# A hand-ordered kernel of gated linear attention and a rational feed-forward: the list of its 800 steps put into another order

## The chip, the core and the metric

The kernel runs on one core of one Trainium2 chip. A core has four engines that compute, each with an instruction queue of its own that is worked off strictly in order: TensorE (PE in the profile; its weight loads are PEld), VectorE (DVE), ScalarE (ACT) and GpSimd (POOL). SyncE (SP) only issues transfers. Transfers (DMA) are issued from SP's and POOL's queues here and are carried by 16 DMA engines. The metric is the device time of one execution in microseconds; lower is better.

## The reference, cut to what matters

```python
f = 1.0 / (1.0 + np.exp(-f_logit))                   # B, H, S, D = 4, 8, 768, 48
for t in range(S):
    state = f[:, :, t, :, None] * state + np.einsum('bhd,bhe->bhde', k[:, :, t], v[:, :, t])
    y[:, :, t] = np.einsum('bhd,bhde->bhe', q[:, :, t], state)
x = y.transpose(0, 2, 1, 3).reshape(B * S, H * D)    # 3072 x 384
h = x @ w_in                                         # 3072 x 2048
P = a[0] + a[1] * h + a[2] * h**2 + a[3] * h**3
Q = 1.0 + abs(b[0]) * abs(h) + abs(b[1]) * h**2
out = (P / (Q + 1e-06)) @ w_out                      # 3072 x 384
```

## The kernel before

The 3072 rows are cut into 12 units of 256 rows (`unit`; unit n is chunk n // 4 of batch n % 4), so units 0 to 3 are the first chunks of the four batches. A unit goes through an attention part and then through a feed-forward part, whose 2048 columns are handled in 16 blocks of 128 columns.

Nothing is scheduled by a framework. The program is the text constant `ORDER`: a list of steps, in the order in which they are issued, and the loop at the end of the kernel calls one small function for each. A step's number is its unit, the next numbers are a range (head pairs 0 to 4 in the attention part, column blocks 0 to 16 in the feed-forward part), `@n` names which of the four PSUM slots (two banks each) it opens, and a last letter picks the engine. Because each engine works in order, the text fixes the order on every engine; a step starts when the step ahead of it on its engine is through and its inputs have come. Beyond the data dependencies a step can carry `^m`, which makes it wait for the instruction that was named with `!m`. The function `behind` adds that wait. `!m` alone costs nothing.

The steps of the attention part, with the engine that does them:

- `ld n f|k|q|v`: loads; v from POOL's queue, the others from SP's. f, k, q and v have three buffers each, so a load waits until unit n - 3 has let go of the buffer. A load in two halves reads two head pairs at a time.
- `ef`, `ls` (ACT): exp of -f and the logarithm of one plus it (lines 294, 299). `cs` (PE, lines 309 to 317): running sums over the rows of a unit by triangular matrices; it also reads the padding columns of the logarithms, and `ind`. `A` (ACT, line 331): exponentials of these sums, for k (`x` = 1) and for q (`x` = 0).
- `xa n x` (line 336): q or k times A, on DVE, or on POOL with the letter p; half a unit is 128x384, a whole one 128x768.
- `T` (PE, line 350): sixteen transposes into PSUM. `Te` (line 360 on ACT with the letter s; without it the last line of the function, a copy on DVE): takes them out to SBUF.
- `sc` (PE) and `mk` (DVE, line 381): scores and their mask. `ic`, `si` (PE) and `st` (DVE, line 464): the new state. `yi`, `yb` (PE, line 394): the output y from the state and from the scores; `vm` (DVE with v, else POOL, line 388) lays out pieces of v for it. `ye` (ACT with s, line 457; else DVE, line 459): y out of PSUM as x.

The steps of the feed-forward part:

- `wi`, `wo`: the two weights, loaded from POOL's queue; `wi a 8 16` is a quarter of the rows of w_in for the upper eight blocks. `ab_` loads a or b from SP's queue; `fa` (DVE, lines 267 to 275) works out nine small coefficients from b, `fr` reads two of them into ScalarE registers, `fb` scales a.
- `h` (PE, line 480): four blocks of x @ w_in, 12 matmuls. `hy` (ACT, line 492): out of PSUM as bf16.
- `sq` (DVE) or `sa` (ACT, line 501): the square. `ab` (DVE, line 505): the absolute value. `zv` (DVE, line 510) or `zd` (a DMA that adds, issued by POOL, line 514): their sum z. `rq` (ACT, line 519): 1 / (z and constants).
- `p1`, `p2` (DVE, lines 529 and 534): two linear terms of the polynomial, `pm` (DVE, line 539) the product with the square, `tv` (DVE, line 547) or `ta` (an adding DMA issued by POOL, line 543) their sum, `gm` (DVE, line 551) the product with 1/z. Each comes in halves (`0 8`, `8 16`, 128x2048) or whole (`0 16`, 128x4096).
- `o` (PE, line 560): four blocks of the product with w_out for 128 rows. `oe` (ACT, line 568): out of PSUM. `so`: the stores, on SP's queue.

`tab` loads one of ScalarE's two function tables. `cu`, `ci`, `cm`, `cz` make constants: `cz 0` and `cz 1` clear the padding columns of the two sets of buffers (lines 250 to 252), `cz 2` makes `ind`, `cz 3` and `cz 4` make two more. `dm` (PE, line 473) is two matmuls of zeros whose product nothing reads.

The last loop, which turns a line of the text into instructions:

```python
made = steps[name](*(int(x.lstrip("@")) if x.lstrip("@").isdigit() else x for x in args))
made = made if isinstance(made, list) else [made]
if hold is not None:
    for i in made:
        behind(i, hold)
if mark is not None:
    marks[mark] = made[-1]
```

Of the kernel before, what the change touches and what calls it, by code (L numbers as in the profile page):

```python
# [29 lines left out]
hy 0 8 12; yi 1 1; xa 2 0 2 4; yb 1 0 2; ab 0 8 16; ic 2 @3; ye 1 s; T 2 @0; p1 0 8 16 !m5; A 3 1; st 2 0  # L30
h 1 12 16 @1; Te 2 s; sq 0 8 16; A 3 0; ld 4 f; si 2 1; sc 2 1 @0; st 2 1; hy 1 12 16; sc 2 0 @2; p2 0 8 16
ld 3 k; ef 5; h 0 4 8 @3; pm 0 8 16; ls 5; ld 6 f; h 0 0 4 @1; tv 0 8 16; hy 0 4 8; xa 3 0 2 4 p ^m1; mk 2 1
h 1 4 8 @3; ld 4 q; ef 4; ld 3 v ^m4; zv 0 8 16 !m7; hy 0 0 4; yb 2 2 4 @0; ls 4; xa 3 0 0 2 p ^m5; h 1 0 4 @1
mk 2 0; hy 1 4 8; ld 7 f; xa 3 1; yb 2 0 2; ef 6; ld 4 k; yi 2 1; sq 0 0 8; T 3 @2; hy 1 0 4; h 1 8 12 @3
# [595 lines left out]
```

## Time and profile before

| what | value |
|---|---|
| three runs | 216.84, 217.03 and 220.1 us; median 217.03 us |
| the profiled execution | 219.54 us in all, 217.8 us of it the span that the profile shows |
| busy time | PE 194.5, DVE 190.6, ACT 187.5, POOL 78.8 us |
| instructions | PE 2901 matmuls, DVE 243, ACT 178, POOL 98 |
| transfers | 43.15 MB at a mean of 198 GB/s |
| granted TensorE clock, mean | 0.99 |

The profiled execution took 2.5 us longer than the median of the runs, and 1.7 us of it lie outside the span. A busy time is the union of an engine's instructions: on DVE and ACT an instruction starts before the one ahead of it is reported as ended, so a difference between two starts is what an instruction costs on a full engine, and it is a little less than its duration. Matmul ends are modelled, so a busy PE need not be at its peak. The idle time in a row stands before the row's instruction, with the instruction or transfer that ended it.

### The profile page before, as it was taken

The numbers are of one execution on the slowest core, as the hardware profiler recorded it, in microseconds if no ns is written. First come the engines' busy times: TensorE is split into PE (matmuls) and PEld (weight loads), VectorE is DVE, ScalarE is ACT, GpSimd is POOL, SyncE is SP. The second block draws the span as 40 slices with busy tenths as digits, with TensorE's granted clock in tenths as the row PEclk, the third lists the DMA queues.
The fourth block names the chain that finished last, engine by engine and source line by source line (L and its number), as shares of the span: only waits on it lengthen the run. The fifth ranks groups of instructions, "written<-read, shape, count | busy, mean of one in ns | idle before, by whom it ended". The sixth has DMA issues, their size and how long they took to land.

```text
span 217.8 us, 6636 instructions
## 1 busy us (share of the span) xinstructions
PE 194.5 (89%) x2901; PEld 138.5 (64%) x2902; DVE 190.6 (88%) x243; ACT 187.5 (86%) x178; POOL 78.8 (36%) x98
## 2 busy tenths in 40 slices
PE   1397699699988899999999999999999999999791
PEld 0355478477756766666678668768677757765440
DVE  4178549999999999999999999999999999979960
ACT  3863639979989999999999999999999999998921
POOL 7050724116394074070260055193553414132000
PEclk9999889999999999999999999999999999999999
DMA  6999997599899979999999999999999999999722
GB/s 171 232 313 168 253 240 189 66 297 182 217 187 178 163 113 200 223 213 191 253 197 164 257 241 243 210 193 204 215 204 199 221 199 215 207 205 199 158 72 72
DMA packets 61820, 43.15 MB, mean 198 GB/s; under 512 B 51424, under 2 KB 56544, under 8 KB 61792
## 3 DMA queue, kind: packets, MB, share of 16 engines
q0 software_dynamic: 20528, 23.86, 66.9%
q1 hardware_dynamic: 41264, 18.88, 33.2%
q8 instruction: 22, 0.36, 0.6%
q14 instruction: 6, 0.05, 0.1%
HBM read 25.17 MB, written 4.72 MB: 137 GB/s over the span
## 4 chain that ended last, share of the span: by engine, by line
PE 54%; DVE 18%; DMA 13%; ACT 8%; issue 4%; POOL 1%; SPq 0%; DVEq 0%; ACTq 0%
PE op L560 19%; PE hp L480 19%; PE y L394 5%; DMA w_in_sb<-in_moe_w_in_dram 4%; DVE g L539 4%; DMA g<-hy 4%; DMA z<-h 4%; PE tp L350 4%; DVE g L551 3%; PE cs L309 3%; DVE scm L381 2%; DVE hy L534 2%; PE sc L373 2%; DMA f<-in_f_logit_dram 2%; ACT A L331 2%
## 5 line engine op out<-in xcount | busy, mean ns | idle before, releaser
L480 PE MATMUL hp<-x,w_in_sb 128*128 128x256 bf16 x576 | 70.9, 276 | 2.4 <-ACT x L457 1.0
L560 PE MATMUL op<-w_out_sb,g 128*128 128x384 bf16 x384 | 69.2, 326 | 1.8 <-DVE g L551 1.8
L480 PEld LDWEIGHTS <-w_in_sb 128*128 128x128 bf16 x576 | 55.7, 99 | 12.8 <-issue 3.1
L492 ACT CAST hy<-hp 128x1024 bf16<-128x1024 f32 x48 | 48.0, 1026 | 6.9 <-PE hp L480 6.9
L560 PEld LDWEIGHTS <-g 128*128 128x128 bf16 x384 | 35.3, 98 | 25.0 <-DVE g L551 3.2
L519 ACT ACTIVATE qi<-z 128x2048 bf16<-128x2048 bf16 (+1 forms) x20 | 45.3, 2267 | 2.1 <-DMA z<-h 1.9
L543 POOL DMA_DIRECT2D g<-hy x15 | 15.3, 1017 | 50.6 <-DVE hy L534 23.1
L381 DVE TENSOR_TENSOR scm<-sc,mask 128x1024 bf16<-128x1024 f32 x24 | 28.9, 1216 | 4.0 <-PE sc L373 3.9
L551 DVE TENSOR_TENSOR g<-g,qi 128x2048 bf16<-128x2048 bf16 (+1 forms) x22 | 28.8, 1315 | 2.1 <-DMA g<-hy 1.6
L539 DVE TENSOR_TENSOR g<-g,h 128x2048 bf16<-128x2048 bf16 (+1 forms) x22 | 30.4, 1394 | 0.0
L514 POOL DMA_DIRECT2D z<-h x20 | 21.6, 1078 | 21.7 <-DVE z L505 11.6
L501 ACT ACTIVATE h<-hy 128x2048 bf16<-128x2048 bf16 x14 | 27.1, 1934 | 0.0
L331 ACT ACTIVATE A<-cs 128x768 f32<-128x768 f32 (+3 forms) x26 | 19.2, 773 | 1.7 <-PE cs L317 1.6
L534 DVE TENSOR_SCALAR hy<-hy,a_sb 128x2048 bf16<-128x2048 bf16 x24 | 19.9, 834 | 0.3
L336 POOL TENSOR_TENSOR qkp<-k,A 128x384 bf16<-128x384 f32 x12 | 12.1, 1012 | 19.8 <-DVE sig L274 8.0
L529 DVE TENSOR_SCALAR g<-hy,a_sb 128x2048 bf16<-128x2048 bf16 (+1 forms) x22 | 18.9, 862 | 0.2 <-PE op L560 0.2
L505 DVE TENSOR_SCALAR z<-hy 128x2048 uint16<-128x2048 uint16 (+1 forms) x23 | 16.1, 707 | 2.6 <-ACT hy L492 2.6
L212 POOL DMA_DIRECT2D v<-in_v_dram x12 | 12.5, 1042 | 15.4 <-DVE qkp L336 7.0
L309 PE MATMUL cs<-lsp,Ui 128*128 128x384 bf16 (+1 forms) x39 | 11.1, 344 | 6.2 <-ACT lsp L299 6.2
L360 ACT COPY T<-tp 128x1024 f32<-128x1024 f32 (+1 forms) x13 | 12.5, 963 | 4.5 <-PE y L394 3.3
L568 ACT ACTIVATE osb<-op 128x768 f32<-128x768 f32 (+1 forms) x13 | 9.9, 762 | 6.1 <-PE op L560 5.6
L394 PE MATMUL y<-scm,v 64*32 64x128 bf16 x384 | 13.2, 218 | 2.0 <-DVE scm L381 2.0
...
## 6 DMA issues: line engine op xcount, KB each, us to landing
...
out_dram<-osb SPq DMA_DIRECT2D x22, 192.0 KB, 4.2
v<-in_v_dram POOLq DMA_DIRECT2D x12, 192.0 KB, 7.3
w_in_sb<-in_moe_w_in_dram POOLq DMA_DIRECT2D x8, 192.0 KB, 9.0
```

Of the source, the lines that this page charges most:

```text
L331: nc.scalar.activation(t, s["cs", a0][:, :, 0:n1], AF.Exp, scale=1.0 if x else -1.0)
L381: return nc.vector.tensor_mul(t, s["sc", g].rearrange("s r a i t -> s (r a) (i t)"), mb)
L394: nc.tensor.matmul(s["y"][32 * a:32 * a + 32, j, kk * C:kk * C + C].rearrange("e (i t) -> e i t", i=2), lhsT, rhs, start=(j, a) not in s[" ...
L480: nc.tensor.matmul(t[:, m - m0, :].rearrange("f (j t) -> f j t", j=UB), w_in_sb[:, kk, m * P:(m + 1) * P], s["x"][:, :, kk, :], start=(kk ...
L492: nc.scalar.copy(fl(big(s, "hy"), m0, m1), fl(s["hp", m0], 0, m1 - m0))
L501: return nc.scalar.activation(fl(big(s, "h2"), m0, m1), fl(big(s, "hy"), m0, m1), AF.Square)
L514: return nc.gpsimd.dma_start(out=fl(big(s, "z"), m0, m1), in_=fl(big(s, "h2"), m0, m1), accum_op=ALU.add)
L519: return nc.scalar.add_instruction(mybir.InstActivation(name=nc.get_next_instruction_name(), func=AF.Reciprocal, ins=[nc.scalar.lower_ap(f ...
L534: return nc.vector.tensor_scalar(fl(big(s, "hy"), m0, m1), fl(big(s, "hy"), m0, m1), a_sb[:, 1:2], a_sb[:, 0:1], op0=ALU.mult, op1=ALU.add)
L539: return nc.vector.tensor_mul(fl(big(s, "g"), m0, m1), fl(big(s, "g"), m0, m1), fl(big(s, "h2"), m0, m1))
L551: return nc.vector.tensor_mul(fl(big(s, "g"), m0, m1), fl(big(s, "g"), m0, m1), fl(big(s, "qi"), m0, m1))
L560: nc.tensor.matmul(s["op", g][:, j, 0:DM], big(s, "g")[:, m, C * j:C * j + C], w_out_sb[:, m, :], start=(s["on", j] == 1), stop=(s["on", j ...
```

## The change

Only the text `ORDER` changes; no function does. It has 795 steps in place of 813, and no computation of the reference is added or dropped. Four kinds of edit are in it:

- The order of nearly all steps is new, on every engine and on SP's and POOL's queues.
- Some steps run on another engine. `Te` goes from 13 on ACT to 9 on ACT and 4 on DVE (`Te 0 2 4`, `Te 1`, `Te 4`, `Te 10`). `vm` on DVE goes from 7 to 4. Squares: DVE 10 to 9, ACT 14 to 15 halves. z sums: DVE 4 to 5, DMA 20 to 19. g sums: DVE 9 to 8, DMA 15 to 16. `xa` on POOL goes from 22 halves to 21.
- Some pairs of half steps become whole ones: `ab` 1 whole before and 5 after, `p1` 2 and 5, `p2` 0 and 4, `pm` 2 and 3, `gm` 2 and 4, `rq` 4 and 7, `xa` on DVE 1 and 4.
- The waits that are written out go from 31 to 34, and the unread products (`dm`) from 4 to 6. The 34 are put so that no product on POOL (`xa ... p`) is meant to run beside a DVE step between SBUF operands.

The diff, cut to the beginning, the end and the lines with the steps named above:

```diff
@@ -17,88 +17,86 @@
 ORDER = """
-cu 1; cz 2; ld 0 f 2 4; cz 0; ld 1 f; cu 0; cz 4; ld 0 f 0 2; dm 3 @0; ld 0 q 0 2; ci; cm; cz 3; ld 0 v; cz 1
-ef 0 2 4; ld 1 k; ld 0 k 0 2; ld 1 v; ab_ b s; ef 0 0 2; ls 0 0 2; ld 0 q 2 4; ls 0 2 4; ef 1; cs 0 2 4 @1
-cs 0 0 2 @2; A 0 1 2 4; ld 0 k 2 4; A 0 0 0 2; ls 1; xa 0 0 0 2; A 0 0 2 4; cs 1 @3; A 0 1 0 2; ld 2 f
-xa 0 1 0 2 !m0; ld 1 q; T 0 0 2 @0; A 1 1; fa; A 1 0; dm 13 @1; xa 1 1 0 2 p ^m0; Te 0 0 2 s; dm 1 @2
-wi 2 8 16; xa 0 0 2 4; ld 3 f; xa 0 1 2 4; wi 0 8 16; vm 1 v; T 0 2 4 @3; wi 3 8 16; xa 1 1 2 4; wi 1 8 16
-ld 2 k; ab_ a s; ef 2; sc 0 0 @1; dm 10 @0; Te 0 2 4 s; mk 0 0; ls 2; sc 0 1 @2; ic 0 @0; xa 1 0 2 4
-xa 1 0 0 2; mk 0 1 !m3; T 1 @3; st 0 0; ld 2 q; yi 0 1 @1; si 0 1; Te 1 s; cs 2 @2; st 0 1; vm 0 v !m1; fr
-ld 2 v ^m1; yb 0 0 2; ef 3; yb 0 2 4; wi 2 0 8; sc 1 1 @0; ld 5 f; ye 0 s; sc 1 0 @3; wi 3 0 8; mk 1 1 !m2
-ls 3; ic 1 @1; wi 0 0 8; A 2 1; wi 1 0 8; mk 1 0 !m4; h 0 8 12 @0; A 2 0; xa 2 1 0 2 p ^m2; st 1 0; si 1 1
-h 0 12 16 @3; xa 2 1 2 4; ld 3 q; fb; st 1 1; cs 3 @2; hy 0 12 16; vm 2 ^m4; xa 2 0 0 2 p ^m3; yb 1 2 4 @1
...
-o 6 0 0 4; rq 8 0 16; sc 11 0 @1; o 6 1 0 4; mk 11 0; o 7 1 8 12; pm 9 8 16; o 7 0 8 12; yb 11 2 4 @2
-pm 8 0 8; yi 11 0; oe 6 0 2 s; yi 11 1; o 7 0 12 16; rq 9 0 8; p1 9 0 8; so 6 0 2; yb 11 0 2; ta 8 0 8
-p2 9 0 8; h 10 4 8 @1; pm 9 0 8; sa 10 8 16; o 7 1 12 16; ab 10 8 16; o 7 0 0 4; ta 9 0 8; p1 10 8 16
-h 10 0 4 @0; ye 11 s; zd 10 8 16; p2 10 8 16; hy 10 4 8; pm 10 8 16; o 7 1 4 8; hy 10 0 4; o 7 0 4 8
-gm 8 8 16; rq 9 8 16; h 11 12 16 @2; tv 10 8 16; h 11 8 12 @1; oe 7 0 2 s; p2 9 8 16; sa 10 0 8
-o 8 1 12 16 @0; so 7 0 2; gm 8 0 8; ta 9 8 16; h 11 0 4 @3; p1 10 0 8; hy 11 8 12; o 8 1 8 12; ab 10 0 8
-hy 11 12 16; gm 9 0 8; o 8 1 4 8; zd 10 0 8; o 8 0 12 16; sa 11 8 16; pm 10 0 8; o 8 0 8 12; o 8 0 4 8
-ab 11 8 16; o 8 0 0 4; hy 11 0 4; p1 11 8 16; zd 11 8 16; o 9 0 4 8 @1; p2 11 8 16; rq 10 8 16; o 8 1 0 4
-gm 9 8 16; h 11 4 8 @2; p2 10 0 8; o 9 1 0 4; oe 8 0 2 s; pm 11 8 16; o 9 0 0 4; hy 11 4 8; so 8 0 2
-o 9 0 12 16; gm 10 8 16; rq 10 0 8; ta 11 8 16; o 9 0 8 12; ab 11 0 8; o 9 1 8 12; tv 10 0 8; o 9 1 4 8
-sa 11 0 8; o 9 1 12 16; p1 11 0 8; o 10 1 8 12 @3; gm 10 0 8; o 10 0 12 16; oe 9 0 2 s; o 10 0 8 12
-rq 11 8 16; zv 11 0 8; so 9 0 2; o 10 1 4 8; o 10 0 4 8; pm 11 0 8; o 10 0 0 4; rq 11 0 8; gm 11 8 16
-o 10 1 0 4; o 10 1 12 16; p2 11 0 8; o 11 0 8 12 @0; oe 10 0 2 s; tv 11 0 8; o 11 1 8 12 @2; so 10 0 2
-o 11 1 12 16; gm 11 0 8; o 11 0 12 16; o 11 0 0 4; o 11 0 4 8; o 11 1 0 4; oe 11 0 1 s; o 11 1 4 8; so 11 0 1
-oe 11 1 2 s; so 11 1 2
+cu 0; cz 3; ld 0 f 0 2; cz 4; dm 3 @0; ld 0 f 2 4; ci; ab_ b s; ld 1 f; cu 1; ld 0 k 2 4; ld 1 v; ld 0 q 2 4
+ld 0 k 0 2; ld 0 v; ef 0 2 4; ef 0 0 2; fa; ls 0 0 2; ld 1 k; cz 0; ef 1; cz 1; cz 2; ls 0 2 4; ls 1
+cs 0 2 4 @1; ld 1 q; cs 1 @2; A 0 0 2 4; fr; cs 0 0 2 @3; A 1 0; ld 2 f; A 0 1 0 2; A 0 1 2 4; A 1 1
+xa 0 1 2 4; ld 4 f; ld 0 q 0 2; xa 0 1 0 2; A 0 0 0 2; vm 1 v; ic 0 @0; xa 0 0 2 4 !m0; vm 0 ^m0; ld 2 k
+T 0 2 4 @1; st 0 0; wi 1 8 16; xa 1 1 2 4; wi 0 8 16; dm 6 @2; xa 1 0; wi 3 8 16; ld 2 q; ef 2; dm 5 @3
+Te 0 2 4; wi 2 8 16; ab_ a s; ls 2; xa 1 1 0 2; dm 13 @2; cm; sc 0 1 @1; xa 0 0 0 2; T 0 0 2 @3; mk 0 1 !m2
+si 0 1; Te 0 0 2 s; ef 4; sc 0 0 @2; ic 1 @1; mk 0 0; cs 2 @3; st 1 0 !m1; T 1 @2; A 2 1; st 0 1; ld 2 v ^m1
+ld 3 f; A 2 0; yi 0 1 @0; yb 0 2 4; Te 1; wi 3 0 8; ls 4; yb 0 0 2; wi 0 0 8; ld 5 f; si 1 1; ye 0 s; xa 2 1
+wi 2 0 8; sc 1 1 @3; sc 1 0 @2; wi 1 0 8; h 0 8 12 @0; mk 1 1; xa 2 0 0 2 p ^m1; fb; h 0 12 16 @3
+xa 2 0 2 4 p ^m2; hy 0 8 12; st 1 1 !m3; mk 1 0; yi 1 1 @1; hy 0 12 16; T 2 @0; yb 1 2 4; sq 0 8 16; Te 2 s
+ld 3 q; ic 2 @2; yb 1 0 2; st 2 0; sc 2 1 @3; ab 0 8 16; si 2 1; ef 3; cs 4 @0; p1 0 8 16; ye 1 s; st 2 1
+ls 3; vm 2 v !m6; mk 2 1; A 4 1; cs 3 @1; ld 4 q; p2 0 8 16; A 4 0; sc 2 0 @2; zv 0 8 16; A 3 0; yb 2 2 4 @3
+ld 3 k; h 0 0 4 @0; A 3 1; mk 2 0; ef 5; h 0 4 8 @1; ld 4 k; xa 3 0 2 4 p ^m2; hy 0 0 4; ld 3 v; ls 5
+xa 3 0 0 2; h 1 4 8 @2; ld 7 f; pm 0 8 16; hy 0 4 8; h 1 8 12 @0; hy 1 4 8; ab 0 0 8; ld 6 q; xa 3 1; sa 0 0 8
...
+cs 6 @1; Te 4 !m7; wo 8 12; si 5 1; tab 1; rq 0 0 16; st 4 1; ld 7 k; sc 4 1 @0; zd 1 0 8; vm 5 v !m14
+dm 1 @3; st 5 1 !m9; vm 4 ^m6; sc 4 0 @3; xa 5 0 0 2 p ^m7; mk 4 1 !m11; h 3 8 12 @2; ld 6 v ^m9; mk 4 0
...
+rq 6 0 16; o 5 1 12 16; Te 10; xa 11 0 0 2 p ^m25; h 8 12 16 @3; zd 7 8 16; pm 7 8 16; sc 10 0 @2; sc 10 1 @0
...
+o 6 1 12 16; sq 9 8 16; h 10 0 4 @2; hy 10 4 8; gm 7 0 16; zd 9 0 8; sc 11 0 @3; rq 8 0 8; zd 9 8 16
+o 6 0 12 16; o 6 0 0 4; vm 11 ^m25; mk 11 0; h 10 12 16 @1; ta 8 8 16; hy 10 0 4; p1 9 0 16; oe 6 0 2 s
+sc 11 1 @3; o 7 0 0 4 @2; rq 8 8 16; so 6 0 2; h 10 8 12 @0; mk 11 1; p2 9 8 16; o 7 0 12 16; sa 10 0 8
+gm 8 0 8; yb 11 0 2 @3; yi 11 1; yb 11 2 4; ab 10 0 8; hy 10 12 16; o 7 0 8 12; p2 9 0 8; zd 10 0 8; o 7 1 4 8
+hy 10 8 12; pm 9 0 16; yi 11 0; o 7 0 4 8; ye 11 s; o 7 1 12 16; rq 9 0 8; o 7 1 0 4; ab 10 8 16; o 7 1 8 12
+ta 9 8 16; tv 9 0 8; o 8 1 0 4 @1; rq 9 8 16; h 11 8 12 @0; p1 10 0 16; oe 7 0 2 s; h 11 12 16 @3; gm 8 8 16
+sa 10 8 16; so 7 0 2; pm 10 0 8; o 8 1 4 8; o 8 0 12 16; hy 11 12 16; p2 10 0 8; o 8 0 8 12; zd 10 8 16
+pm 10 8 16; o 8 1 8 12; hy 11 8 12; o 8 1 12 16; rq 10 0 8; p2 10 8 16; h 11 0 4 @2; p1 11 8 16; ta 10 8 16
+gm 9 0 8; o 8 0 0 4; sa 11 8 16; o 8 0 4 8; gm 9 8 16; h 11 4 8 @3; oe 8 0 2 s; ab 11 8 16; o 9 1 12 16 @0
+hy 11 0 4; pm 11 8 16; so 8 0 2; zd 11 8 16; o 9 0 4 8; hy 11 4 8; p2 11 8 16; o 9 0 8 12; rq 10 8 16
+o 9 1 8 12; tv 10 0 8; ta 11 8 16; o 9 1 4 8; p1 11 0 8; o 9 1 0 4; sa 11 0 8; gm 10 0 8; o 9 0 0 4
+o 9 0 12 16; ab 11 0 8; o 10 1 4 8 @1; gm 10 8 16; oe 9 0 2 s; o 10 0 4 8; o 10 1 0 4; rq 11 8 16; zv 11 0 8
+so 9 0 2; o 10 1 12 16; o 10 0 0 4; p2 11 0 8; o 10 0 12 16; rq 11 0 8; pm 11 0 8; o 10 0 8 12; gm 11 8 16
+o 10 1 8 12; oe 10 0 2 s; tv 11 0 8; o 11 1 12 16 @2; so 10 0 2; o 11 0 12 16 @3; gm 11 0 8; o 11 0 8 12
+o 11 1 8 12; o 11 1 0 4; o 11 1 4 8; o 11 0 4 8; oe 11 1 2 s; o 11 0 0 4; so 11 1 2; dm 15 @0; oe 11 0 1 s
+so 11 0 1
 """
```

More of the change, by code (lines that the diff above doesn't have):

```diff
@@ L30 @@
[L30 to L34, printed above, removed]
```

99 lines of the change are left out of this document (47 added, 52 removed).

## The prediction

> **What bounds the kernel now.** I read the page first: how busy each engine is, where in the span, and what the chain that ended last is made of.
>
> ```profile
> PE 194.5 (89%) x2901; PEld 138.5 (64%) x2902; DVE 190.6 (88%) x243; ACT 187.5 (86%) x178; POOL 78.8 (36%) x98
> ...
> DVE  4178549999999999999999999999999999979960
> ...
> PE 54%; DVE 18%; DMA 13%; ACT 8%; issue 4%; POOL 1%; SPq 0%; DVEq 0%; ACTq 0%
> ```
>
> Three engines are busy for 86 to 89% of the span, and no single one is the bound. The second line shows VectorE full from the seventh slice to the last but two. What is free lies at the two ends, so I asked for the busy time by stretches of 10 us:
>
> ```profile
> 40.00:50.00 10.00, 8.03 (x173) 6.53 (x171) 9.97 (x10) 8.06 (x10) 1.10 (x2) 1.00 0.86 204
> 80.00:90.00 10.00, 10.00 (x175) 7.25 (x174) 10.00 (x13) 9.97 (x10) 3.67 (x4) 1.00 1.13 187
> 180.00:190.00 10.00, 10.00 (x83) 7.81 (x81) 9.89 (x12) 10.00 (x10) 3.14 (x4) 1.00 1.03 211
> ```
>
> The columns are PE, its weight loads, DVE, ACT, POOL. Between 80 and 190 all three are at 96 to 100%: there a better order has little to fill, and only less work on an engine helps it. In the early stretch DVE is full (9.97) while PE has 2 us and ACT 1.9 us free. So I follow VectorE: its time is its start, plus its work, plus what stretches it, plus the last products. The chain of waits, in order of time, gives both ends:
>
> ```profile
> 15.76 9.75 DMA w_in_sb<-in_moe_w_in_dram
> 25.65 2.65 PE hp L480 x12
> ...
> 209.22 1.24 DVE g L551
> 210.50 2.79 PE op L560 x16
> ```
>
> The first feed-forward matmul waits for w_in, which lands at 25.5; VectorE's last product ends at 210.45, and sixteen matmuls, a copy and a store follow. The timeline of ScalarE and VectorE shows when VectorE's feed-forward work begins:
>
> ```profile
> 30.30 1.93 ACT L492 CAST hy<-hp 128x1024 bf16<-128x1024 f32 x2 [4.89 <-PE hp L480]
> ...
> 32.26 0.69 DVE L505 TENSOR_SCALAR z<-hy 128x2048 uint16<-128x2048 uint16 x1 [2.58 <-ACT hy L492]
> ```
>
> After 32.26 VectorE hardly stops until 210.45. The sum below is made against this execution (span 217.8, 219.54 in all); since the median of the runs is 217.03, 2.51 us less, I take the same difference in microseconds from it.
>
> **The change, part by part.**
>
> **Front: when VectorE starts.** Before, two `hy` follow each other from 30.30 although the first block, `h 0 8 12`, was through at about 28.3: `hy 0 12 16` stands first, and it needs the second block. After, `hy 0 8 12` stands first and is done while PE makes the other block. One copy leaves the path: 1.93 / 2 = 0.97, so −1.0, if w_in lands as before. Whether it does is decided by what stands ahead of the `wi` steps on POOL's queue:
>
> ```profile
> 10.47 0.48 PE L309 MATMUL cs<-lsp,Ui 128*128 128x384 bf16 x1 [1.32 <-ACT lsp L299]
> 12.19 1.52 ACT L331 ACTIVATE A<-cs 128x768 f32<-128x768 f32 x2 [0.99 <-PE cs L317]
> 14.03 2.30 POOL L218 DMA_DIRECT2D w_in_sb<-in_moe_w_in_dram  x4
> ```
>
> Before, `cs 1` runs from 10.47 until the `A` behind it starts at 12.19, 1.7 us; two `A` take 1.52, so a whole one costs 0.76 and a half one about 0.4 to 0.5. After, the `wi` stand behind `vm 0`, which waits for `xa 0 0 2 4`. I count: first `cs` from 7.4, for 0.8; `cs 1` until 9.9; on ACT `A 1 0`, two halves, until 11.6; three half `xa` of 0.5 and one `vm` on DVE until 13.4; `vm 0` on POOL until 13.8. That is 14.03 again within 0.3. The loads ahead on SP's queue are the same eleven of units 0 to 4 but for one (f of unit 4 in place of unit 3), so the landing stays near 25.5. I take −1.0; ends −1.4 (`ye 0` and both `hy` early) and the rival's below.
>
> **VectorE's work after that.** Prices by form, busy time and mean ns of one:
>
> ```profile
> L505 DVE TENSOR_SCALAR z<-hy 128x2048 uint16<-128x2048 uint16 x22 | 14.9, 683 | 2.6 <-ACT hy L492 2.6
> L505 DVE TENSOR_SCALAR z<-hy 128x4096 uint16<-128x4096 uint16 x1 | 1.2, 1219 | 0.0
> L529 DVE TENSOR_SCALAR g<-hy,a_sb 128x2048 bf16<-128x2048 bf16 x20 | 16.3, 814 | 0.2 <-PE op L560 0.2
> L529 DVE TENSOR_SCALAR g<-hy,a_sb 128x4096 bf16<-128x4096 bf16 x2 | 2.7, 1337 | 0.0
> L551 DVE TENSOR_TENSOR g<-g,qi 128x2048 bf16<-128x2048 bf16 x20 | 24.3, 1218 | 1.7 <-DMA g<-hy 1.2 <-ACT qi L519 0.4
> L388 DVE COPY vmp<-v 128x256 bf16<-128x256 bf16 x7 | 1.6, 224 | 0.0
> L459 DVE TENSOR_SCALAR x<-y,sig 128x768 bf16<-128x768 f32 x2 | 2.0, 1006 | 0.0
> L381 DVE TENSOR_TENSOR scm<-sc,mask 128x1024 bf16<-128x1024 f32 x24 | 28.9, 1216 | 4.0 <-PE sc L373 3.9
> L360 ACT COPY T<-tp 128x1024 f32<-128x1024 f32 x11 | 11.3, 1031 | 3.5 <-PE y L394 3.3 <-PE tp L350 0.2
> ```
>
> What an instruction costs on a full VectorE is the distance of two starts:
>
> ```profile
> 200.04 0.69 DVE L505 TENSOR_SCALAR z<-hy 128x2048 uint16<-128x2048 uint16 x1
> 200.65 1.22 DVE L547 TENSOR_TENSOR g<-g,hy 128x2048 bf16<-128x2048 bf16 x1
> ```
>
> 0.69 reported, 0.61 to the next start, so I take 0.08 off each instruction. Then:
>
> - Pairs that become whole: four `ab`, each 2 × 0.603 − 1.139 = 0.07, together 0.27; three `p1`, each 2 × 0.734 − 1.257 = 0.21, together 0.63; four `p2`, which had no whole form, at p1's price, 0.84. Sum −1.74. One `pm` and two `gm` more are whole; I cost that at 0, since products gain little beyond the 0.08.
> - One `tv` fewer (the DMA does it): a product of L551's kind, −1.14. One `sq` fewer and one `zv` more cancel.
> - `vm`: five after the front before, three now: −2 × 0.144 = −0.29. The `xa` left for VectorE after the front are 17 halves in both.
> - `Te` on VectorE: four, of which `Te 0 2 4` and `Te 1` lie in the front, where VectorE waits for w_in anyway; `Te 4` and `Te 10` are new work on a full engine. No row shows VectorE copying 2048 bf16 out of PSUM. From below: 1.22, L551's 2048 bf16 in SBUF. From above: its PSUM reads, 768 elements in 1.006 and 1024 in 1.216, a slope of 0.82 ns, so 2048 in 2.06. The upper one is nearer, as it reads PSUM: 2 × 1.98 = +3.96 (from below +2.28).
>
> Work: −1.74 − 1.14 − 0.29 + 3.96 = +0.8; with the cheap `Te`, −0.9. The Trainium skill, "VectorE: DVE Perf Modes", section on the perf-mode tier table, says that a copy with 16-bit data out of PSUM can still run at two elements per cycle; an estimate from its table is 1.22 us, and the sum would be 1.7 us lower by it. No run here shows it.
>
> **What stretches VectorE.** With a POOL product beside it, a VectorE step between SBUF operands is longer:
>
> ```profile
> 35.96 1.42 DVE L534 TENSOR_SCALAR hy<-hy,a_sb 128x2048 bf16<-128x2048 bf16 x1
> 37.30 2.69 DVE L539 TENSOR_TENSOR g<-g,h 128x2048 bf16<-128x2048 bf16 x1
> 64.47 2.68 DVE L539 TENSOR_TENSOR g<-g,h 128x2048 bf16<-128x2048 bf16 x2
> ...
> 37.88 1.02 POOL L336 TENSOR_TENSOR qkp<-q,A 128x384 bf16<-128x384 f32 x1
> ```
>
> Against 0.81, 1.22 and 2 × 1.22 − 0.08 these are 0.61 + 1.47 + 0.32 = 2.4 us too long. The new waits are to keep the two apart; the waits of before slipped three times after the front, so I take half, −1.2 (ends 0 and −2.4). Behind a waiting POOL product stand `zd`, `ta` and loads of v; POOL is at 36%, so I cost that delay at 0, covered by POOL's own idle time; if that cover goes, `rq` is late next.
>
> **The rest.** ACT loses three and a half `Te` of 1.03 (−3.6) and gains one square; this only keeps it beside VectorE. PE's matmuls are the same but for two `dm` of two matmuls each: one ahead of `sc 4 0`, in the early stretch, hidden in PE's 2 us of idle time there, and one behind the last `o`, beside the copy and the store: 0. The tail behind VectorE's last product has the same sixteen matmuls: 0. The moved loads and stores on SP's queue I cost at 0, since every f, k, q of units 5 on is issued units ahead.
>
> Sum: −1.0 + 0.8 − 1.2 = −1.4: 219.54 becomes 218.1, the median 217.03 becomes 215.6. All cheap ends together: −1.0 − 0.9 − 2.4 = −4.3, 212.7.
>
> **The rivals.**
>
> *The cheap ends hold* (`Te` at 1.22 and no product on POOL beside VectorE): 212.7 and, as PE's 2 us of the early stretch fill too, down to 211. For it: every collision has a name in the rows. Against it: PE has no room between 80 and 190.
>
> *The front slips, and it ends slower.* After, `fa` stands on VectorE ahead of the clears `cz 0`, `cz 1` and `cz 2`, and it waits for b, whose load is now third on SP's queue instead of seventh. `cs 0 2 4` reads what these clears fill.
>
> ```profile
> f<-in_f_logit_dram SPq DMA_DIRECT2D x2, 192.0 KB, 3.3
> b_sb<-in_moe_b_dram SPq DMA_DIRECT2D x1, 1.0 KB, 5.8
> a_sb<-in_moe_a_dram SPq DMA_DIRECT2D x1, 2.0 KB, 8.0
> ...
> 7.41 0.80 PE cs L309 x4
> ...
> 3.70 0.17 DVE L250 MEMSET lsp<- 128x128 uint32 x1
> 4.11 0.11 DVE L252 MEMSET vmp<- 128x64 uint32 x1
> ...
> 11.70 0.16 DVE L267 TENSOR_SCALAR bm<-b_sb 128x2 uint32<-128x2 uint32 x1
> 13.03 0.16 DVE L275 SCALAR_TENSOR_TENSOR sig<-bm,sig 128x1 f32<-128x1 f32 x1
> ```
>
> The last column of the transfers is the time from issue to landing. `fa` takes 11.70 to 13.19, 1.5; the clears 0.52 twice and about 0.2. Issued at 1.9, b lands at 5.2 with the 3.3 of the f halves; `fa` ends at 6.7, the clears at 7.9, half a microsecond behind `cs` at 7.4, which the 0.3 and the wait for `xa` can take. With the 5.8 that b itself took it lands at 7.7 and the clears end at 10.4, 3.0 late; with the 8.0 of a, 5.2 late. All of the front, the `wi` too, moves with it: 217.03 + 3.0 − 1.4 = 218.6, or 220.8, and 222 if the collisions stay as well. It is slower than before from a landing 1.4 us later than 5.2 + 0.1, about 6.7. Against it: b's and a's rows come from a queue with several loads ahead, which it does not have there.
>
> *The gain is given back in new waits.* Wide `rq` wait for the later of two halves of z:
>
> ```profile
> L519 ACT ACTIVATE qi<-z 128x2048 bf16<-128x2048 bf16 x16 | 30.8, 1928 | 0.9 <-DMA z<-h 0.6 <-DVE z L510 0.2
> L519 ACT ACTIVATE qi<-z 128x4096 bf16<-128x4096 bf16 x4 | 14.5, 3624 | 1.3 <-DMA z<-h 1.3
> ```
>
> The idle time ahead of four wide ones was 1.3, of sixteen narrow ones 0.9; three wide ones more are 0.8 at 0.33 each. With a PE that cannot follow between 80 and 190 the −1.4 is lost and this added: 217.8. For it: three engines at 96% and more leave no slack for an order that fits a little less well.
>
> **How the numbers follow.** The forecast, faster by less than 2%, 0.45 (own range 213 to 217); the cheap ends 0.10; given back 0.25; the front slips 0.20, of which 0.12 past 2%. Two per cent, 4.3 us, is about what a measurement of this kernel can tell from no change. So faster 0.10, same 0.45 + 0.25 + 0.08 = 0.78, slower 0.12. The time is the likeliest case's, 215.6. The range takes in the front with a's price (220.8) and all but the lowest of the cheap ends: 212.0 to 221.0, leaving out 0.05 below and 0.12 above.
>
> **What would show it.** Right: VectorE's first feed-forward step begins near 31.2; `Te` rows on VectorE of about 2.06; no L534, L539 or L529 far above its mean; VectorE's last product 1.4 earlier than 210.45. Wrong: the first `cs` later than 8.0, w_in landing after 26.5, ACT or PE idle for `rq` or `g` in the middle, or a VectorE with more than some 4 us of idle time after its start.

## The result, and the profile after

| | before | after |
|---|---|---|
| runs on the same chip, median (lowest to highest) | 218.38 us (216.84 to 220.1) | 229.3 us (229.01 to 232.4) |
| the profiled execution, its span | 219.54 us, 217.8 us | 229.02 us, 227.3 us |
| VectorE's first feed-forward step begins | 32.26 | 32.85 |
| VectorE's last product ends | 210.45 | 219.31 |
| from there to the end of the span | 7.39 us | 8.01 us |

The changed kernel is slower: ratio 1.0557, 95% interval 1.0408 to 1.0706. Executions of one kernel differ by up to 4% (after_k10 below: 224.52 to 234.42 us); the medians here take all of them and the ratios leave out the slowest, so the two need not agree. The forecast was 215.6 us in a range of 212 to 221. Of the 9.5 us between the two spans, 8.3 lie between VectorE's first feed-forward step and its last product. The same three lines of the page of after:

```profile
PE 197.8 (87%) x2906; PEld 140.7 (62%) x2906; DVE 199.8 (88%) x227; ACT 186.1 (82%) x172; POOL 82.4 (36%) x100
...
DVE  1386699999999999999999995999999999999650
...
DVE 39%; DMA 20%; ACT 16%; PE 14%; issue 8%; SPq 1%; DVEq 0%; ACTq 0%
```

VectorE is the longest now (199.8 us, 9.2 more, though it has 16 instructions fewer), and it takes over the chain that ended last: 39% of it in place of 18%, and transfers 20% in place of 13%. PE, which was first in the chain before, has 14%. By stretches (columns as before):

```profile
40.00:50.00 10.00, 10.00 (x165) 8.31 (x163) 9.73 (x13) 10.00 (x10) 3.84 (x5) 1.00 0.96 206
80.00:90.00 10.00, 9.73 (x184) 6.92 (x185) 10.00 (x11) 9.96 (x8) 8.27 (x8) 1.00 0.85 190
140.00:150.00 10.00, 6.82 (x73) 4.39 (x72) 9.96 (x9) 8.13 (x6) 6.30 (x7) 1.00 0.60 121
180.00:190.00 10.00, 10.00 (x169) 7.11 (x167) 10.00 (x10) 10.00 (x9) 3.95 (x6) 1.00 1.06 198
```

The early gap that the change could fill is filled: PE goes from 8.03 to 10.00 and ACT from 8.06 to 10.00 between 40 and 50. The loss is later. Between 140 and 150 PE and ACT are free for 3.2 and 1.9 us while VectorE is busy for 9.96. What VectorE does there is in its timeline (all lines of the program are two lower than before):

```profile
145.55 3.21 DVE L537 TENSOR_TENSOR g<-g,h 128x2048 bf16<-128x2048 bf16 x1
...
157.96 3.71 DVE L527 TENSOR_SCALAR g<-hy,a_sb 128x2048 bf16<-128x2048 bf16 x1
161.59 1.21 DVE L359 COPY T<-tp 128x2048 bf16<-128x2048 bf16 x1
```

A product of 1.22 us takes 3.21, and a `p1` of 0.81 takes 3.71. GpSimd's timeline at these places:

```profile
145.77 1.90 POOL L334 TENSOR_TENSOR qkp<-q,A 128x384 bf16<-128x384 f32 x1
...
147.67 1.34 POOL L386 COPY vmp<-v 128x256 bf16<-128x256 bf16 x1
...
158.57 1.63 POOL L334 TENSOR_TENSOR qkp<-q,A 128x384 bf16<-128x384 f32 x1
...
160.13 2.37 POOL L334 TENSOR_TENSOR qkp<-q,A 128x384 bf16<-128x384 f32 x1
161.09 2.37 POOL L334 TENSOR_TENSOR qkp<-k,A 128x384 bf16<-128x384 f32 x1
```

The long steps lie exactly over a product and a copy, and over three products in a row. These are the collisions that the 34 waits are there to keep away. I add up, for every VectorE step, what it took beyond the usual time of its form (the lower of the medians in the two profiles), from the first feed-forward step to the last product:

| us | before | after | difference |
|---|---|---|---|
| start to last product | 178.19 | 186.46 | +8.27 |
| steps longer than usual | 3.48 | 11.32 | +7.84 |
| idle | 3.91 | 5.72 | +1.81 |
| the rest, that is the work | 170.80 | 169.41 | −1.39 |

So the work fell as it was meant to, the idle time rose a little, and the collisions, which the change is built to remove, more than tripled. (Over the whole execution, the front included, after has about 13 us of them; the expectations below say 12.8.)

**Why the waits do not hold.** A wait `^m` only says that a product must not start before the marked step. It keeps a product away from a step only if the marked step is the one just ahead of the place where the product may run. Before, 19 of the 27 products and copies on POOL start less than 0.8 us after their marked step has ended, and lie for the most part beside a `mk`, `st` or `ye`, which read PSUM. After, 6 of 29 do. The other marks had ended 1 to 54 us earlier: `xa 11 0 0 2 p ^m25` starts at 158.57, and its mark, `mk 8 0`, ended at 129.61. Such a wait is over before the product reaches the head of POOL's queue and binds nothing; the product runs when POOL comes to it, beside whatever VectorE is doing. All of the collisions over 0.7 us in after belong to these loose waits. They could have been told from the diff: `vm 11 ^m25` and `xa 11 0 0 2 p ^m25` share one mark and stand far apart.

**The second thing that shows is a transfer.** VectorE's longest idle time after its start, and SP's queue:

```profile
138.68 0.56 DVE L334 TENSOR_TENSOR qkp<-k,A 128x384 bf16<-128x384 f32 x1 [2.62 <-DMA k<-in_k_dram]
```

```profile
101.81 18.00 SPq L575 DMA_DIRECT2D out_dram<-osb  x4
119.90 1.65 SPq L210 DMA_DIRECT2D k<-in_k_dram  x2
121.64 6.29 SPq L210 DMA_DIRECT2D q<-in_q_dram  x1
```

The store `so 2 0 2` stands at the head of SP's queue from 103 until the `oe` that it waits for is through at 118; behind it wait the loads of k of units 11 and 10 and of q of unit 10. k of unit 10 is issued at 120.6 and lands 18 us later, at 138.6, where the loads of k take 7.4 us in the median of this profile; why this one is slow is open. The wait is only 2.62 us because VectorE is itself late by then.

### The profile page after: what moved, and what is told of

Read it like the earlier page. It is cut to its first block, busy times and chain, and to the rows that moved or that the text cites. A ratio compares the mean times of both kernels' runs of the same rounds, so it can differ in the third digit from the quotient of the medians.

```text
span 227.3 us, 6636 instructions
## 1 busy us (share of the span) xinstructions
PE 197.8 (87%) x2906; PEld 140.7 (62%) x2906; DVE 199.8 (88%) x227; ACT 186.1 (82%) x172; POOL 82.4 (36%) x100
## 4 chain that ended last, share of the span: by engine, by line
DVE 39%; DMA 20%; ACT 16%; PE 14%; issue 8%; SPq 1%; DVEq 0%; ACTq 0%
DMA k<-in_k_dram 8%; DMA out_dram<-osb 8%; DVE g L537 7%; PE op L558 5%; DVE scm L379 5%; DVE qkp L334 4%; DVE g L527 4%; DVE g L549 4%; ACT qi L517 3%; PE hp L478 3%; ACT A L329 3%; ACT hy L490 3%; DMA q<-in_q_dram 3%; DVE g L545 3%; DVE h L494 2%
## 5 line engine op out<-in xcount | busy, mean ns | idle before, releaser
L478 PE MATMUL hp<-x,w_in_sb 128*128 128x256 bf16 x576 | 68.5, 273 | 5.2 <-DVE scm L379 5.0
L558 PEld LDWEIGHTS <-g 128*128 128x128 bf16 x384 | 35.5, 98 | 25.3 <-DVE g L549 2.4
L512 POOL DMA_DIRECT2D z<-h x19 | 20.2, 1130 | 38.5 <-ACT hy L490 14.8
L537 DVE TENSOR_TENSOR g<-g,h 128x2048 bf16<-128x2048 bf16 (+1 forms) x21 | 31.5, 1500 | 0.3 <-ACT h L499 0.3
L379 DVE TENSOR_TENSOR scm<-sc,mask 128x1024 bf16<-128x1024 f32 x24 | 28.8, 1210 | 0.5 <-PE sc L371 0.5
L499 ACT ACTIVATE h<-hy 128x2048 bf16<-128x2048 bf16 x15 | 29.0, 1931 | 0.0
L334 POOL TENSOR_TENSOR qkp<-q,A 128x384 bf16<-128x384 f32 x14 | 19.6, 1411 | 18.7 <-ACT A L329 10.2
L527 DVE TENSOR_SCALAR g<-hy,a_sb 128x2048 bf16<-128x2048 bf16 (+1 forms) x19 | 22.8, 1198 | 0.1
L329 ACT ACTIVATE A<-cs 128x784 f32<-128x784 f32 (+3 forms) x26 | 19.1, 780 | 3.4 <-PE cs L315 2.9
L532 DVE TENSOR_SCALAR hy<-hy,a_sb 128x2048 bf16<-128x2048 bf16 (+1 forms) x20 | 18.2, 909 | 0.1
L210 POOL DMA_DIRECT2D v<-in_v_dram x12 | 14.3, 1192 | 10.9 <-DVE state L462 8.1
L334 POOL TENSOR_TENSOR qkp<-k,A 128x384 bf16<-128x384 f32 x7 | 9.9, 1418 | 22.4 <-DVE g L545 11.2
L334 DVE TENSOR_TENSOR qkp<-k,A 128x384 bf16<-128x384 f32 (+1 forms) x14 | 10.6, 765 | 6.9 <-ACT A L329 4.3
```

The costliest lines, as they stand in the source:

```text
L329: nc.scalar.activation(t, s["cs", a0][:, :, 0:n1], AF.Exp, scale=1.0 if x else -1.0)
L334: i = (nc.gpsimd if eng == "p" else nc.vector).tensor_mul(s["qk"][:, x, :, hh, 0:D], s["qk"[x]][:, hh].rearrange("p h i d -> p i h d"), s[ ...
L379: return nc.vector.tensor_mul(t, s["sc", g].rearrange("s r a i t -> s (r a) (i t)"), mb)
L478: nc.tensor.matmul(t[:, m - m0, :].rearrange("f (j t) -> f j t", j=UB), w_in_sb[:, kk, m * P:(m + 1) * P], s["x"][:, :, kk, :], start=(kk ...
L499: return nc.scalar.activation(fl(big(s, "h2"), m0, m1), fl(big(s, "hy"), m0, m1), AF.Square)
L512: return nc.gpsimd.dma_start(out=fl(big(s, "z"), m0, m1), in_=fl(big(s, "h2"), m0, m1), accum_op=ALU.add)
```

## The experiments

Each run is compared with the kernel before on the same chip. The median of the kernel before went from 218.38 to 221.84 us between these chips and times, so compare kernels by the ratio. "Start" is VectorE's first feed-forward step, "rest" the time from there to the end of the span, which takes the noise of the front out at least in part; "collisions" and "idle" are counted as above. The last four columns are of the profiled execution, us. The two profiles of the kernel before (before, before_again) differ by 1.2 us in the rest, so a difference of that size in this column says nothing. In the lines below, the same step stands up to four lines higher or lower in `kernel.py`, as the text `ORDER` is longer or shorter.

| kernel | median us | ratio to before (95%) | start | rest | collisions | idle |
|---|---|---|---|---|---|---|
| before | 218.38 | 1 | 32.26 | 185.6 | 3.5 | 3.9 |
| after | 229.3 | 1.0557 (1.0408 to 1.0706) | 32.85 | 194.5 | 11.3 | 5.7 |
| after_rehold | 226.9 | 1.0281 (1.0192 to 1.0370) | 34.18 | 191.5 | 2.6 | 11.6 |
| after_k10 | 228.82 | 1.0436 (1.0350 to 1.0522) | 29.96 | 195.5 | 10.9 | 7.4 |
| after_rehold_k10 | 219.35 | 1.0045 (1.0005 to 1.0086) | 29.68 | 185.9 | 2.5 | 6.3 |
| after_rk_te | 224.05 | 1.0229 (1.0111 to 1.0346) | 32.30 | 188.4 | 4.2 | 8.5 |
| after_nopool | 235.81 | 1.0683 (1.0577 to 1.0789) | – | – | – | – |
| before_nohold | 227.94 | 1.0378 (1.0307 to 1.0449) | 29.70 | 195.4 | 15.9 | 2.7 |
| before_nopool | 224.68 | 1.0200 (1.0133 to 1.0267) | 35.39 | 189.1 | 2.1 | 1.1 |
| before_rehold | 217.33 | 0.9866 (0.9803 to 0.9929) | 32.42 | 183.9 | 1.9 | 4.0 |
| before_rehold_te | 218.36 | 0.9829 (0.9711 to 0.9948) | 29.69 | 184.8 | 1.5 | 3.0 |
| before_again | 220.13 | one execution | 31.65 | 186.8 | 3.6 | 5.2 |

Theory A: the collisions make the loss. Theory B, the rival: the new order is slower by itself, through its dependencies, and the collisions only fill time in which VectorE would wait. In the edits, steps that are left out stand as `...`.

**after_rehold: the waits made tight.** Thirteen of POOL's steps in the changed kernel wait for the VectorE step directly ahead of one that reads PSUM. No step moves.

```diff
-xa 2 1;  ...  xa 2 0 0 2 p ^m1;  fb;  ...  xa 2 0 2 4 p ^m2
+xa 2 1 !m26;  ...  xa 2 0 0 2 p ^m26;  fb !m27;  ...  xa 2 0 2 4 p ^m27
...
-pm 6 0 8;  ...  xa 10 0 0 2 p ^m22;  ...  tv 6 0 8;  ...  vm 10 ^m23
+pm 6 0 8 !m31;  ...  xa 10 0 0 2 p ^m31;  ...  tv 6 0 8 !m32;  ...  vm 10 ^m32
...
-p1 7 8 16;  ...  xa 11 0 0 2 p ^m25;  ...  pm 7 8 16;  ...  xa 11 0 2 4 p ^m21;  ...  xa 11 1 0 2 p ^m24
+p1 7 8 16 !m33;  ...  xa 11 0 0 2 p ^m33;  ...  pm 7 8 16 !m34;  ...  xa 11 0 2 4 p ^m34;  ...  xa 11 1 0 2 p ^m34
```

> The changed order with only the written-out waits of thirteen POOL steps moved to a VectorE step that stands directly ahead of one that reads PSUM (the product is to run beside that one). Theory A, products on POOL that run beside VectorE steps between SBUF operands make the loss: the time by which VectorE's steps are longer than their usual length falls from 12.8 us to under 4, its first feed-forward step begins near 31.9 instead of 32.85, and the median falls from about 229 to about 220 (218 to 222.5). Theory B, the order's own waits (the late load of k, stores, wide reciprocals) make the loss and would take up any shorter VectorE step: the median stays at 226 or more.

Measured: 226.9 us, in the range of B, and the start is 34.18 in place of the expected 31.9, although the collisions are gone as A says, from 11.3 us to 2.6. Less than that reaches the end: 3 us by the rest, and by the ratios 2.8 of the 5.6 points. VectorE's timeline shows where the rest went:

```profile
141.02 0.56 DVE L334 TENSOR_TENSOR qkp<-k,A 128x384 bf16<-128x384 f32 x1 [5.96 <-ACT hy L490]
```

This is the same `xa` of unit 10, and it now waits for 5.96 us in place of 2.62. The row names `hy`, but that was long through; the load of k was issued at 120.95 and landed at 140.93. So the late load had been hidden under the collisions. The rows of granted clock of after and of after_rehold show that such a wait can cost more than itself:

```profile
PEclk9999799999999999999999999999999999999999
```

```profile
PEclk9988599999999999999999999759999999999999
```

The 7 and 5 in the middle of the second row are 144.4 to 151.2: TensorE, which was busy for 18% of the 3.4 us before, runs at half its clock for 6.8 us. So far neither theory holds by itself.

**before_nohold: the waits taken away.** In the kernel before, POOL's products and copies lose their written waits; the data dependencies stay.

```diff
-xa 1 1 0 2 p ^m0;  ...  vm 2 ^m4;  xa 2 0 0 2 p ^m3
+xa 1 1 0 2 p;  ...  vm 2;  xa 2 0 0 2 p
```

> The order of before without the written-out waits of its POOL products and copies (waits of loads stay). Theory A: POOL products start as soon as their data is there and meet VectorE steps between SBUF operands; the excess of VectorE's steps rises from 3.5 to 8 us or more and the time by 4 to 9 us, to 221 to 226. Theory B: fewer waits, no change or a little faster, 215 to 218.

Measured: 227.94 us, 8.3 more than the kernel before on this chip (219.67), as A says. Collisions rise from 3.5 to 15.9 us, and the rest from 185.6 to 195.4. One of them, the same `p1` form as at 157.96 in after, with two products from 89.07 and one from 90.99 beside it:

```profile
89.99 2.91 DVE L527 TENSOR_SCALAR g<-hy,a_sb 128x2048 bf16<-128x2048 bf16 x1
```

The waits of the kernel before are thus worth some 8 us; by the collisions (11.3 against 3.5 and 15.9) after had lost two thirds of that.

**after_nopool and before_nopool: no products on POOL.** All of POOL's products and copies (21 and 22 halves of `xa`, and the `vm`) go to VectorE, without waits.

```diff
-xa 11 0 0 2 p ^m25;  ...  vm 11 ^m25
+xa 11 0 0 2;  ...  vm 11 v
```

> The changed order with all 21 POOL products and 8 copies done by VectorE at the same place of the text. VectorE gets 21 x 0.47 + 8 x 0.14 = 11.0 us more work and can meet no POOL product. Theory A: the 12.8 us of excess go, so the sum is -1.8 and the median 226 to 231, though VectorE, in order, may wait where POOL waited at no cost. Theory B: 11 us more work on the fullest engine, 238 to 241.

> The order of before with all 22 POOL products and 5 copies done by VectorE: 11.0 us more work, 3.5 us of excess gone. Theory A: +7.5, so about 224 to 227, and the distance between the two orders shrinks from 12 us to between 0 and 6. Theory B: both orders grow by 11, and the distance stays near 12.

Measured: 235.81 and 224.68. The second is as A expects; the first lies between the two. With no product left on POOL to collide with, the changed order is still 11 us behind the old one. So A does not hold alone; something else is slow, the order itself or the places in it at which VectorE now does POOL's products. VectorE's longest waits behind the front in after_nopool follow. They only point, as its profiled execution was the longest of its four (241.59 us; the others took 233.22 to 236.65):

```profile
DVE qkp L332 <- DMA k<-in_k_dram: 7.7, 2, 5.5
DVE g L547 <- ACT qi L515: 3.4, 1, 3.4
DVE z L501 <- ACT hy L488: 3.2, 1, 3.2
```

The longest is the same load of k, 5.5 us at 147.94, and TensorE's clock halves behind it, from 150.7 to 157.6. VectorE's idle time is 15.1 us there and 1.1 in before_nopool; what else makes the 11 us was not taken apart. I changed the theory: A2, collisions and the late load together, each covering for the other. It stands as theory A in the next two expectations.

**after_k10: the load alone.**

```diff
-oe 2 0 2 s;  p2 4 0 16;  ...  so 2 0 2;  ...  ld 11 k;  rq 3 8 16;  ta 4 0 8;  ld 10 k
+oe 2 0 2 s;  p2 4 0 16;  ...  ld 10 k;  so 2 0 2;  ...  ld 11 k;  rq 3 8 16;  ta 4 0 8
```

> One load moved in the changed kernel: the load of k of unit 10 is issued ahead of the store so 2 0 2 instead of behind it. Theory A (collisions of loosely held products and this late load together make the loss): VectorE's wait of 2.62 us for k at 138.68 is gone and the collisions stay, so 226 to 227.5 where the changed kernel has 229.3. Theory B (the changed order is slower by itself, and a wait taken away comes back as another): 228.5 to 230.

Measured: 228.82, the median of five executions from 224.52 to 234.42, in the range of B; the profiled one took 227.16, in that of A. The ratio is 1.0436 in place of 1.0557, and the two intervals overlap. So this run does not tell A from B. In the profile VectorE's wait at 138.68 is gone, but its idle time is 7.4 in place of 5.7: waits in other places have grown, one for `rq 11 8 16` from 1.71 to 2.72.

**after_rehold_k10: both.** The two edits above in one kernel.

> The thirteen products and copies held directly behind a VectorE step as in after_rehold, and the load of k of unit 10 ahead of the store. after_rehold had 2.6 us of collisions left where the changed kernel had 11.3, but waited 5.96 us for k at 141.02, with TensorE at half its clock from 144.4 to 151.2. Theory A: both are gone, 218 to 221, within 2% of the kernel before. Theory B (the order is slower by itself): 225 or more, with VectorE waiting elsewhere.

Measured: 219.35 us, ratio 1.0045 (1.0005 to 1.0086), as A2 says. Nothing of the order has been moved but one load, so B in its plain form falls: of the loss of 5.6%, these two edits take back 5.1. By the ratios the load alone takes back 1.2 points, which is within the noise, and the tight waits alone 2.8; on top of each other they take back 2.4 and 3.9, clear of it. By the rest the load alone gives nothing (+1.0), the tight waits 3.0, and both together 8.6. That each covers for the other is seen in the rows, where the wait for k went from 2.62 to 5.96 as the collisions went; how much that is worth is not shown. The chain in this kernel: the load is issued at 100.08, when SP's queue is free, the `xa` of unit 10 runs at 141.83 without a wait, and TensorE's clock stays whole:

```profile
100.08 0.55 SPq L210 DMA_DIRECT2D k<-in_k_dram  x1
```

```profile
141.83 0.55 DVE L334 TENSOR_TENSOR qkp<-q,A 128x384 bf16<-128x384 f32 x1
142.30 0.55 DVE L334 TENSOR_TENSOR qkp<-k,A 128x384 bf16<-128x384 f32 x1
```

```profile
PEclk9999999999999999999999999999999999999999
```

**before_rehold: the same edit on the kernel before.** Two of its loose waits, those of unit 3 whose rows the prediction shows, cost 0.62 and 1.48 us.

```diff
-tv 0 8 16;  ...  xa 3 0 2 4 p ^m1;  ...  ld 3 v ^m4;  zv 0 8 16 !m7;  ...  xa 3 0 0 2 p ^m5
+tv 0 8 16 !m26;  ...  ld 3 v ^m4;  xa 3 0 2 4 p ^m26;  ...  zv 0 8 16 !m7;  ...  xa 3 0 0 2 p ^m7
```

> The kernel before with only its two loose products of unit 3 held tightly: xa 3 0 2 4 behind tv 0 8 16 and xa 3 0 0 2 behind zv 0 8 16, each directly ahead of a step that reads PSUM; the load of v of unit 3 keeps its time. The steps p2 0 8 16 and pm 0 8 16 lost 0.62 and 1.48 us to them. Theory A (a collision on VectorE's path is lost one for one): 2.1 us faster than the kernel before, ratio 0.99. Theory B (the products come late for the transposes of unit 3, or VectorE only waits later): no difference, ratio 1.00.

Measured: ratio 0.9866 (0.9803 to 0.9929); the rest falls by 1.7 us. VectorE, and the two products on GpSimd:

```profile
36.12 0.80 DVE L534 TENSOR_SCALAR hy<-hy,a_sb 128x2048 bf16<-128x2048 bf16 x1
36.84 1.22 DVE L539 TENSOR_TENSOR g<-g,h 128x2048 bf16<-128x2048 bf16 x1
38.10 1.23 DVE L547 TENSOR_TENSOR g<-g,hy 128x2048 bf16<-128x2048 bf16 x1
39.24 1.22 DVE L381 TENSOR_TENSOR scm<-sc,mask 128x1024 bf16<-128x1024 f32 x1
40.38 1.21 DVE L510 TENSOR_TENSOR z<-z,h 128x2048 bf16<-128x2048 bf16 x1
41.51 1.22 DVE L381 TENSOR_TENSOR scm<-sc,mask 128x1024 bf16<-128x1024 f32 x1
```

```profile
39.47 0.99 POOL L336 TENSOR_TENSOR qkp<-q,A 128x384 bf16<-128x384 f32 x1 [7.28 <-ACT hy L492]
41.67 1.00 POOL L336 TENSOR_TENSOR qkp<-q,A 128x384 bf16<-128x384 f32 x1 [1.21 <-DVE z L510]
```

`p2` and `pm` go from 1.42 and 2.69 to 0.80 and 1.22. The products lie beside the two masks, which read PSUM and keep their 1.22, and take 1.0 us themselves. So here a collision on a full VectorE was lost about one for one (2.1 us expected, 1.7 by the rest, and by the ratio between 0.7 and 2.0%), and the place beside a step that reads PSUM was free.

**after_rk_te and before_rehold_te: the copies `Te 4` and `Te 10`.** The first gives them back to ScalarE in after_rehold_k10, the second gives them to VectorE in before_rehold.

```diff
-Te 4 !m7;  ...  rq 6 0 16;  o 5 1 12 16;  Te 10
+Te 4 s !m7;  ...  Te 10 s;  rq 6 0 16;  o 5 1 12 16
```

```diff
-yb 3 2 4;  Te 4 s;  p1 1 8 16;  ...  pm 7 0 8;  Te 10 s;  o 5 1 12 16
+yb 3 2 4;  Te 4;  p1 1 8 16;  ...  pm 7 0 8;  Te 10;  o 5 1 12 16
```

> after_rehold_k10 with one part of the change undone: the copies Te 4 and Te 10 are ScalarE's again (Te 10 ahead of rq 6 0 16). Each costs VectorE 1.22 us and ScalarE about 1.03. Theory A (VectorE is the bound, and what it is relieved of shows one for one): 2.4 us less than after_rehold_k10, so 216 to 218 where that has 219.4. Theory B (ScalarE, busy for 26 to 29 of each 30 us, is as full, so the copies only change sides): 219 to 221.

> One part of the change done alone, on before_rehold: the copies Te 4 and Te 10 on VectorE instead of ScalarE. In after_rk_te, ScalarE taking them back cost about 4 us instead of saving 2.4. Theory A (VectorE is the bound in the kernel before, idle for 4 us of 178 there, and each copy costs it 1.22): 2.4 us more than before_rehold, ratio 1.00. Theory B (ScalarE is as full, and what it is relieved of makes up for it): as before_rehold or less, ratio 0.985.

Measured: 224.05 in place of 219.35, where A expected 2.4 less and B no difference: worse than both. The second: ratio 0.9829 against 0.9866, intervals that overlap, where A expected 1.00; B holds. ScalarE in after_rk_te:

```profile
59.71 1.01 ACT L358 COPY T<-tp 128x1024 f32<-128x1024 f32 x1 [0.51 <-PE tp L348]
60.74 1.28 ACT L288 ACT_TABLE_LOAD   x1
62.03 3.62 ACT L517 ACTIVATE qi<-z 128x4096 bf16<-128x4096 bf16 x1
65.67 1.28 ACT L288 ACT_TABLE_LOAD   x1
66.96 0.82 ACT L329 ACTIVATE A<-cs 128x784 f32<-128x784 f32 x1
```

`Te 4` waits 0.51 for its transposes, and the table, the wide `rq`, the second table and the next `A` queue behind it. In after_rehold_k10 that `rq` starts at 59.52 and that `A` at 64.45, both 2.5 us earlier; 1.0 of this was there before the copy (the `hy` ahead of it starts at 57.18 and 58.18), and 1.5 is the copy and its wait. VectorE, whose first feed-forward step came 2.62 later in this profile, has caught up by 60 (`st 4 1` at 59.85 and 59.87) and falls 4.5 us behind between 77 and 85: `mk 5 1` waits 1.57 for its scores, and `tv 1 8 16` takes 4.01 in place of 1.22 under two products:

```profile
81.45 4.01 DVE L545 TENSOR_TENSOR g<-g,hy 128x2048 bf16<-128x2048 bf16 x1
```

These products start 1.9 and 1.4 us later than in after_rehold_k10, because the `zd` ahead of them on POOL's queue waited 1.33 us for ScalarE's square. From there VectorE stays 4 to 6 us behind, 5.1 at the end. By the table its rest is 2.5 us longer: 2.2 more idle time and 1.7 more collisions, for 1.4 less work. So ScalarE is as full as B says, and its lateness reaches VectorE through POOL's queue too; that this one place makes nearly the whole loss is read from one profile and not tested.

**before_again: the kernel before, a second profile.**

> The kernel before, unchanged, for a second profile: whether the first feed-forward step of VectorE, at 32.26 us in the first profile, moves with the stretch of half TensorE clock that stood at 25.8 to 29.2 there. Theory A (that stretch is what differs between profiles of one program): without such a stretch ahead of it the step begins near 30; with one, near 32. Theory B (the order of the front sets it): 32.2 either way.

Measured: 220.13 us, start 31.65, with a half-clock stretch from 25.4 to 28.8. As A expects of a profile with a stretch; as it was there again, the run does not tell A from B. What does is the start column beside the clock of each profile: without a half-clock stretch between 20 and 30 us the start is 29.69 and 29.70 in kernels with the front of before (before_rehold_te, before_nohold) and 29.68 and 29.96 with that of after (after_rehold_k10, after_k10); with one of 3.4 us it is 31.65 to 32.42 and 32.30 to 32.85; with one of 6.8 us and one of 3.4 ahead of it, 34.18 (after_rehold). The kernels without products on POOL, whose front has other work, are left out.

## Why the prediction was wrong, step by step

- **"What stretches VectorE", −1.2: the step that failed.** I named the mechanism and priced it from its rows, then credited the new waits with half of it because they are meant to keep the two apart, and set the ends at 0 and −2.4, with no room for a loss. It was +7.8. I had the 34 waits in the diff and did not set each mark beside its product; 23 of 29 stand too far apart to bind. The price was there too: before, eight loose ones cost 3.25 us over the whole execution, 0.41 each; 23 at that price are 9.4, 6.1 more than before, and with the other terms of the sum 222.9 us. That was the rival to write, and none of the three was it.
- **"The moved loads and stores on SP's queue I cost at 0": failed too.** The loads are issued in an order that is units ahead, but what a load waits for is the store in front of it on the same queue, and that waits for `oe`. It cost 2.62 us in the open, and 5.96 with a half-clock stretch behind it once the collisions were gone; taking it away on top of the tight waits was worth 2.4 points.
- **"Behind a waiting POOL product … covered by POOL's own idle time": right,** for the tight waits. In after_rehold_k10, with 13 more tight waits, nothing of that shows: 219.35.
- **`Te` on VectorE: the lower end held.** Against the 2.06 that I took:

```profile
L359 DVE COPY T<-tp 128x2048 bf16<-128x2048 bf16 x3 | 3.7, 1220 | 1.9 <-ACT lsp L297 1.9
L527 DVE TENSOR_SCALAR g<-hy,a_sb 128x2048 bf16<-128x2048 bf16 x14 | 14.2, 1017 | 0.0
L527 DVE TENSOR_SCALAR g<-hy,a_sb 128x4096 bf16<-128x4096 bf16 x5 | 8.5, 1705 | 0.1
```

  1.220 us, the lower end, and the estimate from the table of the Trainium skill, "VectorE: DVE Perf Modes", which I had set beside the sum and not in it. The nearest row in kind (a PSUM read) was the wrong neighbour: those rows are 32-bit sources. And relieving ScalarE, which I set at 0 as "this only keeps it beside VectorE", is worth something by after_rk_te and before_rehold_te. The two `L527` rows show collisions from a group's mean: 1017 and 1705 ns where before had 814 and 1337.
- **VectorE's work, +0.8:** −1.39 measured. With `Te` at 1.22 the sum gave −0.9; the pairs, the `tv` and the `vm` were sized about right.
- **Front, −1.0:** +0.59. That the first `hy` comes 1.74 earlier is mostly the clock's doing: in the profile of before a half-clock stretch lies over the first `h` block (2.65 us in place of 1.48), in that of after it is over by then. In profiles without one, the first `hy` starts at 27.73 and 27.75 in the order of before (before_rehold_te, before_nohold) and at 27.33 and 27.60 in that of after (after_rehold_k10, after_k10). The copy has left the path, but the first block starts 1.4 to 1.6 us later (25.82 and 26.10 in place of 24.46 and 24.48), which I had not in the step. Moreover VectorE's first step there squares both blocks, and the second comes late in after, by a collision again:

```profile
26.33 2.78 DVE L334 TENSOR_TENSOR qkp<-k,A 128x768 bf16<-128x768 f32 x1
```

```profile
28.56 1.01 ACT L490 CAST hy<-hp 128x1024 bf16<-128x1024 f32 x1 [1.69 <-PE hp L478]
31.80 1.01 ACT L490 CAST hy<-hp 128x1024 bf16<-128x1024 f32 x1 [2.23 <-PE hp L478]
```

```profile
30.30 1.47 PE L478 MATMUL hp<-x,w_in_sb 128*128 128x256 bf16 x12 [1.77 <-DVE scm L379]
```

  `xa 2 1` takes 2.78 in place of 0.95 beside two products, the mask behind it is late, and PE, waiting 1.77 for it, makes the second block late. With that gone and no half-clock stretch both fronts start within 0.3 us of 29.7: the order of the front alone is worth nothing that these runs show.
- **Tail, 0:** +0.62. I counted sixteen matmuls behind the last product, as before. In after PE has all 32 matmuls of unit 11 to do from 216.84, where the `gm` ahead of the last one ends, late, as it waits 1.71 for `rq 11 8 16`; that `rq` stands behind an `oe` that waits 2.79 for the store of unit 8 to let go of the output buffer. But the matmuls end 2.96 us behind the last product, before 2.83, which is 0.14 of the 0.62. The rest is stores: the two last copies end 0.77 us apart in place of 1.24, and their four stores are issued one behind the other on SP's queue, the last 1.08 us after the copy in place of 0.61. The chain of waits of after:

```profile
213.68 1.91 ACT qi L517
215.62 1.24 DVE g L549
216.90 5.39 PE op L558 x32
```

- **The rivals.** The front did not slip: b landed early, `fa` ran from 5.08, and the first `cs` stands at 7.81, inside the 8.0. Given back in new waits: the idle time rose by 1.81, about its size, but by a load and the wait for `rq 11 8 16`, and it was the smaller part. The cheap ends: `Te` was cheap, the other was not.
- **The list of what would show it** named the right signs: L527, L532 or L537 far above their means, and more than 4 us of idle time.
- **Two readings that were off,** without weight in the sum: ScalarE is at 94%, not 96%, between 170 and 180 us, and three wide `rq` at 0.33 are 1.0 us, not 0.8, unless the idle time of the narrow ones is taken off.
